# Attention, Mish MoE and SwiGLU MoE in one kernel: another order and other tiles for the conversion of the second MoE's weights

## The chip, the core and the metric

The kernel runs on one core of a Trainium2 chip. The metric is the device time of one execution in microseconds, median of the runs. The core has five engines with a queue of instructions each: TensorE (PE in the profile), VectorE (DVE), ScalarE (ACT), GpSimd (POOL) and SyncE (SP), which here issues every DMA. Each queue runs in the order in which the program wrote it; queues wait for one another only where a tile makes them.

## The reference

```python
def _attn_ref(q, k, v):            # 4 x 8 heads x 576 x 64; local heads and strided heads
...
    attn = attn / (np.sum(attn, axis=-1, keepdims=True) + 1e-09)
    return np.matmul(attn, v).astype(np.float32)

def _moe_ref(x, w_in, w_out):      # 2304 tokens, 512 -> 2048 -> 512
    h = x @ w_in
    sp = np.where(h > 20.0, h, np.log1p(np.exp(np.minimum(h, 20.0))))
    g = h * np.tanh(sp)
    return (g @ w_out).astype(np.float32)

def _moe2_ref(x, w_gate, w_val, w_out):   # 512 -> 1536 -> 512
    g = x @ w_gate
    silu = g * (1.0 / (1.0 + np.exp(-g)))
    val = x @ w_val
    return (silu * val @ w_out).astype(np.float32)
```

The weights come as 64-bit floats. The kernel itself turns them into 32-bit ones.

## The kernel before

**Precision.** Every operand of the two MoEs is held as two parts, hi (the value rounded to the matmul's type, by ScalarE, `split_hi`) and lo (the rest, a subtraction, `split_lo`), and each product is three matmuls (`mm3`): hi hi, hi lo, lo hi.

**Phases.** Attention runs first, its units interleaved with the start of MoE 1. MoE 1 is cut in 20 steps n = 0 to 19 (4 quarters of the hidden width by 5 chunks of tokens; four chunks have 512 tokens, the fifth, n = 4, 9, 14 and 19, has 256). Step n runs the first product of chunk n (`h`, four groups f of 12 matmuls each) and then the second product of chunk n-1 (`y`, 48 matmuls in four groups). The hidden PSUM tiles have the tag `mm` with three buffers, so group f = 3 needs the buffer that the Mish of group f = 0 (L436, ScalarE, out `u`) has read. After the second product four additions (L477, L479, `y_out`) go to VectorE. After step 19 come twelve rounds of MoE 2 (tiles `c..`, then `o`), which read their weights back from DRAM (`ld`, L555).

**Conversion of weights.** `wlist` holds 32 weight tiles of MoE 1 and 60 of MoE 2 (36 read from the input, 24 sums or differences `S12`, `S34` of tiles already converted). One unit of conversion is `w_unit`. For a tile read from the input it is: a Square of the high word on ScalarE (L183), four operations a, b, c, d on VectorE (L184, L187, L190, L193; d needs the Square), and the DMA that loads the raw tile of the unit two raw units on (`w_load`, L130; the tag `raw` has two buffers). For an S tile it is two half operations on VectorE (L165 and L171, or L167 and L174). Later `w_flush` makes the hi part (ScalarE, L74) and the lo part (GpSimd, L79), and for MoE 2 the DMA that stores both to DRAM (L142). For MoE 1 the parts stay in a tile of tag `w`; for MoE 2 they are built in a staging tile of tag `ws`, which has two buffers. The Square is written into the second half of the same tile, where the lo part comes later:

```python
    nc.scalar.activation(out=w[:, 1], in_=hi.bitcast(F32), func=AF.Square)
```

`w_unit` begins with `w_flush(1)`: unit k flushes all but the newest pending tile, so hi, lo and store of tile k-2 are written out ahead of the Square and of a to d of tile k.

**Where units stand.** Steps 3 to 17 of MoE 1 hold 82 units, 22 for MoE 1 and 60 for MoE 2 (`W1_STEP`, `W2_STEP`), placed after the groups of the two products by `bg`. `act_c` puts the hi part of the hidden values on ScalarE after each `y` group and its lo part on GpSimd (tile `g`). At the end of each step `w_flush()` makes the parts of all that is pending.

**Other tiles in the change.** `v` tiles of attention have four buffers (`NV`); the load of unit u+4 is issued after the product of unit u (`at_v`). In the rounds, the two hidden tiles of the last chunk (`fs4`) use the same tag. The output weights of each round (`p`) are loaded at the end of that round into tag `raw` (two buffers), and used by the `o` matmuls one round later.

Of the kernel before, what the change touches and what calls it, by code (L numbers as in the profile page):

```python
# [7 lines left out]
F32 = mybir.dt.float32  # L8
F32R = mybir.dt.float32r
# [3 lines left out]
ALU = mybir.AluOpType  # L13
# [32 lines left out]
    (2, 0, 18), (2, 1, 19), (2, 2, 20), (2, 3, 21), (3, 0, 21), (3, 1, 21), (3, 2, 21), (3, 3, 21),  # L46
)
WSTEPS = (0, 0, 1, 1, 1, 1, 1, 1, 1, 1, 1, 1, 1, 1, 1, 1) + (1, 2) * 6 + (0,) * 20
NV = 4
WF = 8  # L50
DO2 = 6

# [2 lines left out]
def local_strided_attention__mish_moe__swiglu_kernel(  # L55
# [22 lines left out]
    def split_lo(eng, lo, src, hi):  # L78
        eng.tensor_tensor(out=lo, in0=src, in1=hi.bitcast(F32), op=ALU.subtract)  # L79
# [52 lines left out]

    wpend = []

    def w_flush(keep=0):
        while len(wpend) > keep:
            key, w, tf = wpend.pop(0)
            split_hi(nc.scalar, w[:, 0], tf)
            split_lo(nc.gpsimd, w[:, 1], tf, w[:, 0])
            if len(key) == 3:  # L140
                wd[key] = dram.tile([128, 2, 512], F32, name="wd_%s_%d_%s" % key)
                nc.sync.dma_start(wd[key], w.bitcast(F32))  # L142

    def w_ops():
        i = wpos[1]
        if i >= len(wlist):
            return []
        wpos[1] += 1
        key, src = wlist[i]
        if len(key) == 2:  # L150
            t = sb.tile([128, 512], I32, tag="wtmp", name="wtmp", bufs=2)
            w = sb.tile([128, 2, 512], F32R, tag="w", name="w", bufs=10)
            wt[key] = w
        else:
            t = sb.tile([128, 512], I32, tag="pt", name="wt2", bufs=6)
            w = sb.tile([128, 2, 512], F32R, tag="ws", name="ws", bufs=2)
        tf = t.bitcast(F32)
        if src is None:
            t0, t1 = (f32[key[:2] + (x,)] for x in ("W0", "W1"))
            f32[key] = tf  # L160
            lo, hi = slice(0, 256), slice(256, 512)

            def s1():
                if key[2] == "S12":
                    nc.vector.tensor_tensor(out=tf[:, lo], in0=t1[:, lo], in1=t1[:, hi], op=ALU.add)  # L165
                else:
                    nc.vector.tensor_tensor(out=tf[:, lo], in0=t0[:, lo], in1=t1[:, lo], op=ALU.subtract)  # L167

            def s2():
                if key[2] == "S12":  # L170
                    nc.vector.tensor_tensor(out=tf[:, hi], in0=tf[:, lo], in1=t0[:, lo], op=ALU.subtract)  # L171
                else:
                    s = f32[key[:2] + ("S12",)]
                    nc.vector.tensor_tensor(out=tf[:, hi], in0=t0[:, hi], in1=s[:, hi], op=ALU.subtract)  # L174
                wpend.append((key, w, tf))

            return [s1, s2]
        raw = raws.pop(i).bitcast(I32).rearrange("p (n t) -> p n t", t=2)
        lo, hi = raw[:, :, 0], raw[:, :, 1]
        f32[key] = tf  # L180

        def a():
            nc.scalar.activation(out=w[:, 1], in_=hi.bitcast(F32), func=AF.Square)  # L183
            nc.vector.tensor_scalar(t, hi, 3, 0x3FFFFFFF, op0=ALU.logical_shift_left, op1=ALU.bitwise_and)  # L184

        def b():
            nc.vector.scalar_tensor_tensor(t, lo, 29, t, op0=ALU.logical_shift_right, op1=ALU.bitwise_or)  # L187

        def c():
            nc.vector.scalar_tensor_tensor(t, hi, -0x40000000, t, op0=ALU.bitwise_and, op1=ALU.bitwise_or)  # L190

        def d():
            nc.vector.scalar_tensor_tensor(tf, w[:, 1].bitcast(F32), SMALL2, tf, op0=ALU.is_ge, op1=ALU.mult)  # L193
            wpend.append((key, w, tf))
            w_load()

        return [a, b, c, d]
# [9 lines left out]
                wq.pop(0)()  # L207

    def w_unit():
        w_flush(1)  # L210
        for do in w_ops():
            do()


    pairs = [(b, hp) for b in range(B) for hp in ((0, 1, 2, 3) if b < B - 1 else (2, 3, 0, 1))]
# [3 lines left out]
        for j in range(0, nb, st_):  # L219
            units.append((i, b, hp, list(range(j, min(j + st_, nb)))))  # L220
    NU = len(units)
    qk_t, v_t = {}, {}
    st = {}

    def load_qk(i):
# [5 lines left out]

    def load_v(u):
        i, b, hp, js = units[u]
        t = sb.tile([128, 4, 128], F32, tag="v", name="v", bufs=NV)
        v_t[u] = t = t[:LK if hp < 2 else 128, :len(js)]
        nc.sync.dma_start(t, (v_loc if hp < 2 else v_str)[2 * b + hp % 2, u % 3, :, :len(js)])

# [132 lines left out]
            load_qk(i + 2)  # L370

    def at_v(u):
        if u + NV < NU:
            load_v(u + NV)

    DENSE = [
        [
# [67 lines left out]
    def do(n=None):  # L445
        for _ in range(len(todo) if n is None else min(n, len(todo))):
            todo.pop(0)()
# [52 lines left out]
    def g2_by_f(n, after, banks=PS4):  # L500
        nt = CHUNKS[n % NCH][1]
        y = [ps.tile([128, 512], F32, tag=t, name="y", bufs=k)[:, :nt] for t, k in banks]
        for f in range(QF):
            for e in range(4):
                g2_mm(n, y[e], e, f)
            after(f)
        for e in range(4):
            y_out(n, y[e], e)
# [35 lines left out]
    def ld(r, *what):  # L544
        if r >= 2 * NP:
            return
        P, i = divmod(r, NP)
        for x in what:
            for kind in "p" if x in (0, 1) else "gv":
                tag, n = TAGS[x]  # L550
                ws[kind, r, x] = t = sb.tile([128, 2, 512], F32R, tag=tag, name="wr", bufs=n)
                if x == "W1" and P == 1:
                    nc.sync.dma_start(t[:, :, 256:].bitcast(F32), wd[kind, i, x][:, :, 256:])
                else:
                    nc.sync.dma_start(t.bitcast(F32), wd[kind, i, x])  # L555
# [8 lines left out]
        ("X", "W1", 1, "T4"),  # L564
    ]
    BANK = {"g": {"X": ("mm", 3), "Y": ("mm", 3), "Z": ("mm", 3)}, "v": {"X": ("sc", 2), "Y": ("xp", 2), "Z": ("tp", 1)}}
    fv, fs = {}, {}

    def finish(r, f, c, w=512):
        t = fv.pop((r, f, c))  # L570
        if w == 512:
            h = sb.tile([128, 2, 512], F32R, tag="g", name="fs", bufs=6)
        else:
            h = sb.tile([128, 2, 256], F32R, tag="v", name="fs4", bufs=NV)
        split_hi(nc.scalar, h[:, 0], t)
        split_lo(nc.gpsimd, h[:, 1], t, h[:, 0])
        fs[r, f, c] = h
# [85 lines left out]
    with tc.manual_schedule():  # L663
# [75 lines left out]
        for n in range(3, NA):  # L739
            q, c = divmod(n, NCH)  # L740
            units = W1_STEP.get(n, 0) + W2_STEP.get(n, 0)
            left = [units, 8]

            def bg(k):
                while left[0] * 8 > units * k:
                    left[0] -= 1
                    w_unit()

            for f in range(QF):
                g1_open(n, f)  # L750
                for kc in range(4):
                    g1_mm(n, f, kc)
                act_a(n, f, False)
                bg(7 - f)
                if n == NA - 2 and f % 2:
                    operand(0, ("B11", "T1")[f // 2])

            def after(f):
                act_c(n, f)
                do()  # L760
                bg(3 - f)
                if n == NA - 2:
                    operand(0, ("T2", "B22", "T3", "B21")[f])
                if n == NA - 1 and f == 0:
                    operand(0, "T4")

            if n == NA - 1:
                w_flush()
                ld(0, "S34", "W0", "S12", "W1", 0, 1)
            g2_by_f(n - 1, after)  # L770
            w_flush()
        g2_by_f(NA - 1, lambda f: None, [("mm", 3), ("mm", 3), ("mm", 3), ("tp", 1)])
        for r in range(2 * NP + 1):
            P = r // NP
            if r < 2 * NP:
                ld(r + 1, "W0")

                def between(n):
                    if n == 2:
                        ld(r + 1, "S12")  # L780
                    if n == 4:
                        ld(r + 1, "S34")
                    if r == NP - 2 and n == 6:
                        operand(1, "B11")
                    if r == NP - 1 and n < 6:
                        operand(1, ("T1", "T2", "B22", "T3", "B21", "T4")[n])

                c_round(r, between)
            if r > 0:
                for t in range(4):  # L790
                    d_tile(r - 1, 1, t)
            if r < 2 * NP:
                finish(r, 0, 0)
                finish(r, 1, 0)
                if P == 0:
                    c4_round(r)
                ld(r + 1, "W1")
            if r > 0:
                for t in range(4):
                    d_tile(r - 1, 0, t)  # L800
                if r <= NP:
                    for t in range(2):
                        d_tile(r - 1, 4, t)
            if r > 0:
                ld(r, 0, 1)


_INS = ["qk", "v_loc", "v_str", "w1", "w2", "consts"]
# [86 lines left out]
```

## Time and profile before

| | |
|---|---|
| median of 3 runs | 992.34 us (987.35 to 992.46) |
| the profiled execution | 987.49 us, span 985.7 us |
| PE busy | 925.3 us (94%) |
| DVE busy | 616.2 us (63%) |
| ACT busy | 383.6 us (39%) |
| POOL busy | 374.4 us (38%) |
| mean granted TensorE clock | 0.967 |

The span is the time from the first to the last instruction. Busy shares are means over phases that differ: attention until about 166 us, steps 3 to 19 of MoE 1 until 561 us, then the rounds. A line number is a line of the kernel; all matmuls of the MoEs have one line (L83) and all hi and lo parts two (L74, L79), so tiles tell them apart.

### The profile page before, as it was taken

What the parts mean: (1) busy time and instruction counts of PE and PEld (TensorE: products, weight loads), DVE (VectorE), ACT (ScalarE), POOL (GpSimd) and SP (SyncE); (2) the same over time, 40 slices, a digit from 0 to 9 for tenths busy, and PEclk for the clock granted to TensorE, in tenths of its full rate; (3) what the DMA queues carried; (4) which work ended last, traced back from release to release, by engine and by line L of the source; (5) the groups of instructions that cost most, each with busy time, mean ns of one, the idle gap of its engine ahead of it and who ended that gap; (6) DMA issues with size and microseconds to landing.
All of it is one profiled execution on the core that took longest, in us unless ns stands there. A gap on an engine that the chain in (4) does not pass through costs nothing.

```text
span 985.7 us, 13926 instructions
## 1 busy us (share of the span) xinstructions
PE 925.3 (94%) x4982; PEld 767.8 (78%) x4987; DVE 616.2 (63%) x1232; ACT 383.6 (39%) x951; POOL 374.4 (38%) x303
## 2 busy tenths in 40 slices
PE   8998999997988969899599999999999899999997
PEld 6776887885867858678488888888887788888885
DVE  5896567698978989798886434333346343334433
ACT  5667646353434433443435343213224222322230
POOL 3345134664746646474556422021034221112210
PEclk9989999998989979899799999999999999999999
DMA  8774421454555455554442632523514246443313
GB/s 305 241 247 166 143 95 53 171 171 156 200 178 175 167 170 190 185 196 152 154 168 96 249 111 103 213 66 149 213 43 171 73 184 250 176 172 106 128 44 128
DMA packets 48501, 156.72 MB, mean 159 GB/s; under 512 B 5296, under 2 KB 11824, under 8 KB 48432
## 3 DMA queue, kind: packets, MB, share of 16 engines
q1 hardware_dynamic: 48432, 155.83, 44.9%
q8 instruction: 39, 0.64, 0.3%
q14 instruction: 30, 0.25, 0.1%
HBM read 119.64 MB, written 36.18 MB: 158 GB/s over the span
## 4 chain that ended last, share of the span: by engine, by line
PE 48%; ACT 2%; DVE 1%; issue 0%; DMA 0%; POOL 0%; ACTq 0%; POOLq 0%
PE o L83 15%; PE cXg L83 6%; PE cXv L83 6%; PE y L83 5%; PE c L83 4%; PE h L83 3%; PE cZv L83 3%; PE cZg L83 3%; PE cYv L83 2%; PE cYg L83 2%; ACT T L74 0%; DMA wr<-wd_p 0%; DVE T L79 0%; DVE B L79 0%; DVE k L616 0%
## 5 line engine op out<-in xcount | busy, mean ns | idle before, releaser
L83 PE MATMUL h<-xh,w 128*128 128x512 f32 (+1 forms) x640 | 210.3, 397 | 38.4 <-ACT u L436 38.0
L83 PE MATMUL y<-g,w 128*128 128x512 f32 (+1 forms) x960 | 208.0, 372 | 0.0
L83 PEld LDWEIGHTS y<-g,w 128*128 128x128 f32 x960 | 167.0, 190 | 29.8
L83 PEld LDWEIGHTS h<-xh,w 128*128 128x128 f32 x640 | 123.7, 200 | 64.1 <-ACT u L436 40.9
L83 PE MATMUL o<-wr,fs 128*128 128x512 f32 x648 | 152.3, 393 | 5.9 <-DMA wr<-wd_p 3.1
L79 POOL TENSOR_TENSOR fs<-k,fs 128x512 fp32r<-128x512 f32 x36 | 47.0, 1306 | 279.1 <-ACT fs L74 243.6
L83 PEld LDWEIGHTS o<-wr,fs 128*128 128x128 f32 x648 | 122.1, 189 | 32.4 <-DVE s L616 3.2
L79 POOL TENSOR_TENSOR g<-u,g 128x512 fp32r<-128x512 f32 (+1 forms) x80 | 111.4, 1399 | 83.8 <-ACT g L74 83.5
L83 PE MATMUL h<-xl,w 128*128 128x512 f32 (+1 forms) x320 | 124.1, 388 | 0.0
L659 DVE TENSOR_TENSOR acc<-acc,o 128x512 f32<-128x512 f32 x90 | 61.7, 687 | 62.4 <-PE o L83 62.4
L79 POOL TENSOR_TENSOR ws<-wt,ws 128x512 fp32r<-128x512 f32 x60 | 86.4, 1449 | 33.2 <-ACT ws L74 33.1
L278 ACT ACTIVATE pt<-pt,sm 108x64 f32<-108x64 f32 (+1 forms) x160 | 55.8, 350 | 50.1 <-DVE sm L263 49.8
L83 PEld LDWEIGHTS h<-xl,w 128*128 128x128 f32 x320 | 64.4, 201 | 9.2 <-DVE xl L79 0.3
L293 POOL TENSOR_TENSOR pt<-pt,sm 128x288 f32<-128x288 f32 (+2 forms) x48 | 37.1, 772 | 89.8 <-DVE sm L292 74.7
L183 ACT ACTIVATE ws<-raw 128x512 fp32r<-128x512 f32 x36 | 24.1, 670 | 118.4 <-issue 32.7
L603 DVE TENSOR_TENSOR k<-cZg,k 128x512 f32<-128x512 f32 x12 | 8.3, 691 | 98.4 <-PE cZg L83 98.4
L79 POOL TENSOR_TENSOR w<-wtmp,w 128x512 fp32r<-128x512 f32 x32 | 48.1, 1504 | 46.4 <-ACT w L74 40.4
L193 DVE SCALAR_TENSOR_TENSOR wt<-ws,wt 128x512 f32<-128x512 f32 x36 | 37.4, 1038 | 44.3 <-ACT ws L183 42.5
L74 ACT CAST fs<-k 128x512 fp32r<-128x512 f32 x36 | 22.4, 622 | 91.6 <-PE o L83 40.1
L83 PE MATMUL cXg<-T,wr 128*128 128x512 f32 x216 | 54.9, 390 | 0.4 <-DVE k L603 0.4
L83 PE MATMUL cXv<-T,wr 128*128 128x512 f32 x216 | 54.8, 389 | 0.0
L74 ACT CAST ws<-wt 128x512 fp32r<-128x512 f32 x60 | 36.3, 620 | 46.8 <-DVE wt L193 10.7
(96 smaller groups left out, 1526.3 us busy)
## 6 DMA issues: line engine op xcount, KB each, us to landing
raw<-in_w_dram SPq DMA_DIRECT2D x68, 512.0 KB, 3.7
qk<-in_qk_dram SPq DMA_DIRECT2D x16, 898.0 KB, 6.4
wr<-wd_g_S SPq DMA_DIRECT2D x24, 512.0 KB, 5.9
wr<-wd_v_S SPq DMA_DIRECT2D x24, 512.0 KB, 5.8
wr<-wd_p SPq DMA_DIRECT2D x24, 512.0 KB, 4.0
wr<-wd_g_W SPq DMA_DIRECT2D x18, 512.0 KB, 5.8
wr<-wd_v_W SPq DMA_DIRECT2D x18, 512.0 KB, 6.5
wd_g_W<-ws SPq DMA_DIRECT2D x12, 512.0 KB, 2.6
```

What stands on the lines that cost most here:

```text
L74: nc.scalar.copy(hi, src)
L79: eng.tensor_tensor(out=lo, in0=src, in1=hi.bitcast(F32), op=ALU.subtract)
L83: nc.tensor.matmul(o, lhsT=lhs, rhs=rhs, start=first and i == 0, stop=last and i == 2, skip_group_check=more)
L183: nc.scalar.activation(out=w[:, 1], in_=hi.bitcast(F32), func=AF.Square)
L193: nc.vector.scalar_tensor_tensor(tf, w[:, 1].bitcast(F32), SMALL2, tf, op0=ALU.is_ge, op1=ALU.mult)
L278: nc.scalar.activation(out=pt[:, jj], in_=pt[:, jj], func=AF.Exp, scale=-1.0, bias=sm[:, 0, jj:jj + 1], accum_out=sm[:, 1, jj:jj + 1],)
L293: nc.gpsimd.tensor_tensor(out=pt, in0=pt, in1=r.unsqueeze(2).to_broadcast([n, nb, w]), op=ALU.mult)
L603: nc.vector.tensor_tensor(out=t, in0=p, in1=t, op=ALU.add)
L659: nc.vector.tensor_tensor(out=acc[c][:, t], in0=acc[c][:, t], in1=o, op=ALU.add)
```

## The change

1. MoE 2's staging tiles alternate between the tags `ws` and `v`, two buffers each. The tag `v` now has two buffers of twice the size; attention's v tiles use them in pairs, and both loads of a pair (units u+3 and u+4) are issued after the product of an odd unit u. `fs4` tiles are paired in the same way.
2. For MoE 2 the Square goes to a scratch tile of its own, `sq`, of tag `pt`.
3. `w_unit` now begins with `w_lo(nc.vector)` and `w_hi()`: unit k writes out lo and store of tile k-2, then hi of tile k-1, then the Square and a to d of tile k.
4. In `w_unit`, and in the flushes from step 3 on, the lo part is on VectorE, for MoE 1's tiles too. The flushes during attention keep GpSimd.
5. The flush at the end of each step becomes `w_done()`, which flushes only if a tile of MoE 1 is pending; it is also called between the two products.
6. The `p` weights of the last round go to tag `w` and are loaded one round earlier.

```diff
@@ -46,7 +46,6 @@
     (2, 0, 18), (2, 1, 19), (2, 2, 20), (2, 3, 21), (3, 0, 21), (3, 1, 21), (3, 2, 21), (3, 3, 21),
 )
 WSTEPS = (0, 0, 1, 1, 1, 1, 1, 1, 1, 1, 1, 1, 1, 1, 1, 1) + (1, 2) * 6 + (0,) * 20
-NV = 4
 WF = 8
 DO2 = 6
 
@@ -132,14 +131,26 @@
 
     wpend = []
 
-    def w_flush(keep=0):
+    whalf = []
+
+    def w_lo(eng):
+        while whalf:
+            key, w, tf = whalf.pop(0)
+            split_lo(eng, w[:, 1], tf, w[:, 0])
+            if len(key) == 3:
+                wd[key] = dram.tile([128, 2, 512], F32, name="wd_%s_%d_%s" % key)
+                nc.sync.dma_start(wd[key], w.bitcast(F32))
+
+    def w_hi(keep=0):
         while len(wpend) > keep:
             key, w, tf = wpend.pop(0)
             split_hi(nc.scalar, w[:, 0], tf)
-            split_lo(nc.gpsimd, w[:, 1], tf, w[:, 0])
-            if len(key) == 3:
-                wd[key] = dram.tile([128, 2, 512], F32, name="wd_%s_%d_%s" % key)
-                nc.sync.dma_start(wd[key], w.bitcast(F32))
+            whalf.append((key, w, tf))
+
+    def w_flush(keep=0, eng=nc.gpsimd):
+        w_lo(eng)
+        w_hi(keep)
+        w_lo(eng)
 
     def w_ops():
         i = wpos[1]
@@ -153,7 +164,7 @@
             wt[key] = w
         else:
             t = sb.tile([128, 512], I32, tag="pt", name="wt2", bufs=6)
-            w = sb.tile([128, 2, 512], F32R, tag="ws", name="ws", bufs=2)
+            w = sb.tile([128, 2, 512], F32R, tag=("ws", "v")[i % 2], name="ws", bufs=2)
         tf = t.bitcast(F32)
         if src is None:
             t0, t1 = (f32[key[:2] + (x,)] for x in ("W0", "W1"))
@@ -178,9 +189,11 @@
         raw = raws.pop(i).bitcast(I32).rearrange("p (n t) -> p n t", t=2)
         lo, hi = raw[:, :, 0], raw[:, :, 1]
         f32[key] = tf
+        sq = w[:, 1].bitcast(F32) if len(key) == 2 else sb.tile([128, 512], F32, tag="pt", name="sq", bufs=6)
+        sqo = w[:, 1] if len(key) == 2 else sq
 
         def a():
-            nc.scalar.activation(out=w[:, 1], in_=hi.bitcast(F32), func=AF.Square)
+            nc.scalar.activation(out=sqo, in_=hi.bitcast(F32), func=AF.Square)
             nc.vector.tensor_scalar(t, hi, 3, 0x3FFFFFFF, op0=ALU.logical_shift_left, op1=ALU.bitwise_and)
 
         def b():
@@ -190,7 +203,7 @@
             nc.vector.scalar_tensor_tensor(t, hi, -0x40000000, t, op0=ALU.bitwise_and, op1=ALU.bitwise_or)
 
         def d():
-            nc.vector.scalar_tensor_tensor(tf, w[:, 1].bitcast(F32), SMALL2, tf, op0=ALU.is_ge, op1=ALU.mult)
+            nc.vector.scalar_tensor_tensor(tf, sq, SMALL2, tf, op0=ALU.is_ge, op1=ALU.mult)
             wpend.append((key, w, tf))
             w_load()
 
@@ -207,9 +220,14 @@
                 wq.pop(0)()
 
     def w_unit():
-        w_flush(1)
+        w_lo(nc.vector)
+        w_hi()
         for do in w_ops():
             do()
+
+    def w_done():
+        if any(len(x[0]) == 2 for x in wpend + whalf):
+            w_flush(0, nc.vector)
 
 
     pairs = [(b, hp) for b in range(B) for hp in ((0, 1, 2, 3) if b < B - 1 else (2, 3, 0, 1))]
@@ -219,7 +237,7 @@
         for j in range(0, nb, st_):
             units.append((i, b, hp, list(range(j, min(j + st_, nb)))))
     NU = len(units)
-    qk_t, v_t = {}, {}
+    qk_t, v_t, v_p = {}, {}, [None]
     st = {}
 
     def load_qk(i):
@@ -231,7 +249,9 @@
 
     def load_v(u):
         i, b, hp, js = units[u]
-        t = sb.tile([128, 4, 128], F32, tag="v", name="v", bufs=NV)
+        if u % 2 == 0:
+            v_p[0] = sb.tile([128, 2, 4, 128], F32, tag="v", name="v", bufs=2)
+        t = v_p[0][:, u % 2]
         v_t[u] = t = t[:LK if hp < 2 else 128, :len(js)]
         nc.sync.dma_start(t, (v_loc if hp < 2 else v_str)[2 * b + hp % 2, u % 3, :, :len(js)])
 
@@ -370,8 +390,10 @@
             load_qk(i + 2)
 
     def at_v(u):
-        if u + NV < NU:
-            load_v(u + NV)
+        if u % 2:
+            for x in (u + 3, u + 4):
+                if x < NU:
+                    load_v(x)
 
     DENSE = [
         [
@@ -547,7 +569,7 @@
         P, i = divmod(r, NP)
         for x in what:
             for kind in "p" if x in (0, 1) else "gv":
-                tag, n = TAGS[x]
+                tag, n = TAGS[x] if kind != "p" or r < 2 * NP - 1 else ("w", 10)
                 ws[kind, r, x] = t = sb.tile([128, 2, 512], F32R, tag=tag, name="wr", bufs=n)
                 if x == "W1" and P == 1:
                     nc.sync.dma_start(t[:, :, 256:].bitcast(F32), wd[kind, i, x][:, :, 256:])
@@ -564,14 +586,16 @@
         ("X", "W1", 1, "T4"),
     ]
     BANK = {"g": {"X": ("mm", 3), "Y": ("mm", 3), "Z": ("mm", 3)}, "v": {"X": ("sc", 2), "Y": ("xp", 2), "Z": ("tp", 1)}}
-    fv, fs = {}, {}
+    fv, fs, f4 = {}, {}, [None]
 
     def finish(r, f, c, w=512):
         t = fv.pop((r, f, c))
         if w == 512:
             h = sb.tile([128, 2, 512], F32R, tag="g", name="fs", bufs=6)
         else:
-            h = sb.tile([128, 2, 256], F32R, tag="v", name="fs4", bufs=NV)
+            if f == 0:
+                f4[0] = sb.tile([128, 2, 2, 256], F32R, tag="v", name="fs4", bufs=2)
+            h = f4[0][:, f]
         split_hi(nc.scalar, h[:, 0], t)
         split_lo(nc.gpsimd, h[:, 1], t, h[:, 0])
         fs[r, f, c] = h
@@ -765,10 +789,11 @@
                     operand(0, "T4")
 
             if n == NA - 1:
-                w_flush()
+                w_flush(0, nc.vector)
                 ld(0, "S34", "W0", "S12", "W1", 0, 1)
+            w_done()
             g2_by_f(n - 1, after)
-            w_flush()
+            w_done()
         g2_by_f(NA - 1, lambda f: None, [("mm", 3), ("mm", 3), ("mm", 3), ("tp", 1)])
         for r in range(2 * NP + 1):
             P = r // NP
@@ -801,8 +826,10 @@
                 if r <= NP:
                     for t in range(2):
                         d_tile(r - 1, 4, t)
-            if r > 0:
+            if 0 < r < 2 * NP - 1:
                 ld(r, 0, 1)
+            if r == 2 * NP - 2:
+                ld(r + 1, 0, 1)
 
 
 _INS = ["qk", "v_loc", "v_str", "w1", "w2", "consts"]
```

## Rows read from the trace of the kernel before

**Rows 1.** The page: busy time of TensorE, and in 40 equal slices the busy tenths of TensorE and VectorE.

```profile
PE 925.3 (94%) x4982; PEld 767.8 (78%) x4987; DVE 616.2 (63%) x1232; ACT 383.6 (39%) x951; POOL 374.4 (38%) x303
...
PE   8998999997988969899599999999999899999997
...
DVE  5896567698978989798886434333346343334433
```

**Rows 2.** Busy time of each engine in stretches: three single steps of MoE 1 (n = 5, 6 and 7), step 16, and last the whole of steps 3 to 17. Columns: from:to, its length, then busy us and (instructions) of PE, PEld, DVE, ACT and POOL, then the granted clock, the DMA share and GB/s.

```profile
205.13:221.76 16.63, 16.63 (x97) 14.76 (x96) 15.63 (x20) 7.76 (x14) 8.07 (x7) 1.00 0.50 159
221.76:253.13 31.37, 24.39 (x99) 19.66 (x97) 26.30 (x30) 11.35 (x21) 18.00 (x13) 0.89 0.46 151
253.13:274.89 21.76, 21.76 (x98) 18.02 (x96) 20.77 (x23) 8.43 (x15) 14.24 (x10) 1.00 0.61 218
...
460.27:495.11 34.84, 24.75 (x99) 19.86 (x97) 28.13 (x30) 11.07 (x20) 18.68 (x13) 0.80 0.44 151
...
166.71:517.15 350.44, 312.46 (x1441) 261.04 (x1440) 299.71 (x337) 140.25 (x259) 206.07 (x144) 0.93 0.49 172
```

**Rows 3.** Who waited for whom in steps 3 to 17: TensorE's one row, ScalarE's longest with its Square, VectorE's. Columns: total us, times, longest us.

```profile
PE h L83 <- ACT u L436: 38.0, 7, 10.1
...
ACT ws L183 <- issue: 32.7, 8, 5.3
ACT ws L183 <- DMA wd_p<-ws: 30.2, 3, 10.2
...
ACT ws L183 <- DMA raw<-in_w_dram: 17.5, 10, 2.9
...
DVE wt L193 <- ACT ws L183: 39.6, 17, 4.6
```

**Rows 4.** One such wait in order of time, step 16. Columns: start us, length us, engine, line, operation, out<-in, and in brackets the idle time before it and what ended it.

```profile
462.00 1.66 DVE L190 SCALAR_TENSOR_TENSOR wt<-raw,wt 128x512 int32<-128x512 int32 x1
...
464.18 0.36 SPq L142 DMA_DIRECT2D wd_p<-ws  x1
...
469.38 0.66 ACT L183 ACTIVATE ws<-raw 128x512 fp32r<-128x512 f32 x1 [9.90 <-DMA wd_p<-ws]
...
470.07 0.69 DVE L193 SCALAR_TENSOR_TENSOR wt<-ws,wt 128x512 f32<-128x512 f32 x1 [3.82 <-ACT ws L183]
...
478.07 0.59 ACT L436 ACTIVATE u<-h 128x512 f32<-128x512 f32 x1
...
478.72 0.79 PE L83 MATMUL h<-xh,w 128*128 128x512 f32 x1 [10.10 <-ACT u L436]
```

**Rows 5.** VectorE in order of time where GpSimd does nothing beside it: the first S12 halves, and one whole raw unit and the start of the next.

```profile
177.24 0.42 DVE L165 TENSOR_TENSOR wt<-wt 128x256 f32<-128x256 f32 x1
...
178.71 0.42 DVE L184 TENSOR_SCALAR wt<-raw 128x512 int32<-128x512 int32 x1
...
212.64 0.42 DVE L184 TENSOR_SCALAR wtmp<-raw 128x512 int32<-128x512 int32 x1
213.09 0.69 DVE L187 SCALAR_TENSOR_TENSOR wtmp<-raw,wtmp 128x512 int32<-128x512 int32 x1
...
215.23 0.42 DVE L184 TENSOR_SCALAR wtmp<-raw 128x512 int32<-128x512 int32 x1
```

**Rows 6.** Beside GpSimd: one stretch in which VectorE runs nine SBUF operations and GpSimd seven lo parts (columns as in rows 2), and GpSimd's and VectorE's groups of instructions in steps 3 to 17. Columns of a group: line, engine, operation, shape, count | busy us, mean ns of one | idle before.

```profile
247.12:258.94 11.82, 11.82 (x54) 9.79 (x53) 11.58 (x9) 3.97 (x7) 10.25 (x7) 1.00 0.43 150
...
L79 POOL TENSOR_TENSOR ws<-wt,ws 128x512 fp32r<-128x512 f32 x58 | 83.9, 1454 | 33.2 <-ACT ws L74 33.1
L79 POOL TENSOR_TENSOR g<-u,g 128x512 fp32r<-128x512 f32 x50 | 75.7, 1519 | 72.2 <-ACT g L74 72.2
L79 POOL TENSOR_TENSOR w<-wtmp,w 128x512 fp32r<-128x512 f32 x24 | 36.9, 1538 | 37.4 <-ACT w L74 31.4 <-PE h L83 5.6
...
L479 DVE TENSOR_TENSOR acc<-acc,y 128x512 f32<-128x512 f32 x36 | 22.2, 679 | 0.0
```

**Rows 7.** The nearest rows to a lo part on VectorE: in the rounds a VectorE operation with two SBUF inputs of the same size, and the lo parts of MoE 2's operands, each of which runs next to one on GpSimd (steps 18 and 19).

```profile
L616 DVE TENSOR_TENSOR k<-k,k 128x512 f32<-128x512 f32 x36 | 25.5, 708 | 4.1 <-DVE k L603 0.5
...
L79 DVE TENSOR_TENSOR B<-acc,B 128x512 fp32r<-128x512 f32 x3 | 3.9, 1316 | 3.1 <-ACT B L74 3.1
```

**Rows 8.** DMA issues by kind (KB each, median us from issue to landing), and for attention's v tiles the least, median and longest time to landing with the products of a unit and of the unit three later.

```profile
raw<-in_w_dram SPq DMA_DIRECT2D x68, 512.0 KB, 3.7
...
wr<-wd_g_S SPq DMA_DIRECT2D x24, 512.0 KB, 5.9
...
wd_p<-ws SPq DMA_DIRECT2D x12, 512.0 KB, 2.8
...
DMA to landing us min/median/max: 2.1/3.4/6.5
...
48.41 0.57 PE L334 MATMUL xp<-ts,v 96*64 96x64 f32 x12
...
57.68 0.91 PE L334 MATMUL xp<-ts,v 96*64 96x64 f32 x12
```

**Rows 9.** The end: TensorE's wait for the last round's output weights and what it ran then, and the stretch from the last `o` of round 10's weights to the end (columns as in rows 2).

```profile
968.79 1.37 PE L83 MATMUL o<-wr,fs 128*128 128x512 f32 x3 [2.65 <-DMA wr<-wd_p]
970.63 11.35 PE L83 MATMUL o<-wr,fs 128*128 128x512 f32 x45 [0.47 <-DMA wr<-wd_p]
...
966.16:985.70 19.54, 12.72 (x48) 9.64 (x48) 6.19 (x9) 0.00 (x0) 0.00 (x0) 0.91 0.44 161
```

## The prediction

> **What bounds the kernel now.** I read the page first [rows 1]: TensorE is busy 94% of the span, so only its idle and slow stretches can be won. The slices show where they are: between the 10th and the 20th, tenths of 5 to 8 lie beside full ones, and there VectorE stands at 7 to 9, while in the rounds behind it has mostly 3 to 6. That stretch is steps 3 to 17, the steps with units of conversion. I then cut it into single steps [rows 2]. A step without trouble takes 16.6 us when one of its products is of the short chunk (n = 4, 5, 9, 10, 14, 15) and 21.8 us otherwise: 6 x 16.63 + 9 x 21.76 = 295.6 us for the fifteen. They took 350.4, an excess of 54.8. The view of waits names 38.0 of it [rows 3]: TensorE stands seven times at the fourth group of a first product, because ScalarE has not yet read the PSUM tile of the first. The other 16.8 is the clock: in the disturbed steps the granted clock is 0.80 and 0.89 [rows 2], so part of the matmuls after such a wait run at 1.2 instead of 2.4 GHz, and each waited us costs 1.44 us (54.8 / 38.0).
>
> Why ScalarE is late is seen in order of time [rows 4]. Its queue stands 9.9 us at one Square, which writes into a staging tile that must first be stored. The store is issued at 464.2, after two things: the lo part on GpSimd, and the load ahead of it in SP's queue, which waits for operation c on VectorE. The Square starts 5.2 us after the issue. The Mish that TensorE needs is queued behind that Square and a second such one. The same Square holds VectorE, 39.6 us in 17 waits [rows 3].
>
> But VectorE is the second limit. In steps 3 to 17 it is busy 299.7 us [rows 2], and its own work is far less. A raw unit alone takes 215.23 - 212.64 = 2.59 us, two S units (178.71 - 177.24) / 2 = 0.74 each [rows 5]; the additions take 0.68 each [rows 6], 2.7 for a step (1.7 where the chunk is short). 58 x 2.59 + 24 x 0.74 + 12 x 2.7 + 3 x 1.7 = 205 us. The other 95 us are VectorE operations made longer by GpSimd's: 0.66 us for each of 144 GpSimd operations. Where VectorE has no pause it is more: in the stretch of 11.8 us [rows 6] its nine operations would take 4.9 us alone (four of 0.69, five of 0.42) and took 11.6, so 0.96 for each of seven.
>
> The Trainium skill, page "SBUF — State Buffer", section "Who interferes with whom", states this as a lock: a VectorE operation with two SBUF inputs and a GpSimd operation that reads SBUF block each other for a whole instruction. The rows agree: 0.69 alone, 1.66 beside GpSimd.
>
> **The change part by part.**
>
> *The Square's wait* goes. The scratch `sq` was last read by an earlier unit, three or more back by my count through the six `pt` buffers, and hi of tile k now meets a staging tile whose store was issued two units before, against 2.8 us to landing [rows 8]. What is late next is VectorE: hi of tile k-1 now stands at the head of unit k on ScalarE and waits for d of the unit just before, where `w_flush(1)` left one unit more. Behind it are queued the Square, the Mish and the hi parts of `g`. So TensorE will now wait for VectorE's lag alone, and the sum is VectorE's.
>
> *The lo parts.* 82 leave GpSimd. On VectorE one is not seen in these steps; the bounds are 0.7 (two SBUF inputs, same size) and 1.32 (always beside GpSimd) [rows 7]. I take 0.7 and count GpSimd's part separately, since GpSimd keeps only the 62 lo parts of `g`. For those the bounds are 0.66 and 0.96 each; VectorE will have few pauses, but some meet the additions, so 0.8.
>
> *VectorE by step*, against TensorE's 21.76 or 16.63. Raw unit 2.59 + 0.7 = 3.29, S unit 1.44, four `g` 3.2 (2.0 for the short chunk). `w_done` between the products makes VectorE wait for a hi part just issued; ScalarE's operations take about 0.6 [rows 4], some of it covered, 0.4 us in the eight steps that have it.
> - n = 6, 8, 11, 13, 16 (four raw, two S): 13.16 + 2.88 + 2.7 + 3.2 + 0.4 = 22.3, 0.6 too long. n = 7, 12 without the 0.4: 0.2.
> - n = 4, 9, 14 (three raw, two S): 9.87 + 2.88 + 2.7 + 2.0 = 17.4, 0.8 too long.
> - n = 5, 10 (five raw): 16.45 + 1.7 + 3.2 + 0.4 = 21.8, 5.1 too long. n = 15 (six raw): 25.0, 8.4.
> - n = 3 and 17 have room.
>
> The lag adds up to 5 x 0.6 + 2 x 0.2 + 3 x 0.8 + 2 x 5.1 + 8.4 = 24.4 us by step 16. TensorE doesn't feel the first 9: the Mish of the first group is due 3/8 of a long step in, 8.2 us, and ScalarE must have only d of the last unit but one by then (3.3 earlier), less three operations of its own (0.66 + 0.59 [rows 4] and a hi of that size). 15.4 us of waits remain, times 1.44 for the clock 22.2. Steps 3 to 17 take 295.6 + 22.2 = 318 us, 32.6 less. At steps 10 and 15 the lo of the last MoE 1 tile, now behind the additions on VectorE, lets only some 4 us of lag through; what is waited there is not waited later, and the sum stays.
>
> *The last weights.* Their slots in `w` are those of round 10's S12, done by then; SP's queue has only round 10's weights ahead. From 966.16 to 981.98 TensorE ran 48 matmuls [rows 9]; at 21.76 / 96 each [rows 2] they take 10.9. 4.9 us less.
>
> *Costed at nothing.* Attention's v loads: the first of a pair is issued three units ahead, not four; three units took 9.3 us, the longest load 6.5 [rows 8]. Without that cover, say behind a later product, at most 2 us a pair. `fs4` in pairs: the same bytes and order. SP's queue: the store of tile k-2 waits for a lo that VectorE does ahead of a of unit k, so the load behind it, which waits for c, is not held. ScalarE has as many operations as before. The pending tiles at step 19: two lo parts, 1.4 us, in steps that have room.
>
> The profiled execution took 987.5 us, as the lowest of three runs; the median is 992.3. 987.5 - 32.6 - 4.9 = **950.0 us**, which I keep for the median too.
>
> **The rivals.**
>
> *TensorE alone bounds.* If a `g` costs VectorE 0.66 and the wait after `w_done` is covered, the thirteen steps 4 to 16 are 0.56 shorter each (7 us) and eight of them another 0.4 (3 us): lag 14, 5 above what is let through, 7 with the clock. 54.8 - 7 + 4.9 = 53 less, 935; with nothing left, 928. For it: GpSimd's operations will bunch behind the second product, near the additions. Against: the saturated stretch, 0.96.
>
> *The raw loads.* There are still two raw tiles, and each load waits for c of the unit two before: 3.7 to landing and some 2 of a to c and issue is 6 us for two raw units, where VectorE needs 6.6. If landing rises to the 5.9 of the `wr` loads, issued several at a time [rows 8], it is 8.2, 0.8 a unit: over the 16 raw units of steps 5, 10 and 15, 13 us, times 1.44: 969. For it: ScalarE waited 17.5 us for raw tiles already [rows 3]. Against: only in ten short waits.
>
> *Slower.* If VectorE's lost time does not leave with GpSimd's operations, because a moved lo takes 1.32 like the rows beside GpSimd, its work grows by 82 x 0.62 = 51 us. 73 of these units lie in steps 4 to 16: lag 24.4 + 45, less 9, times 1.44 is 87 us: 295.6 + 87 = 383, 32 above now; less the tail's 4.9, 1015. It decides where a lo costs VectorE over 1.0: there the extra lag passes 22.6 us, times 1.44 the whole 32.6. Against: `k<-k,k`, 0.71, has both inputs in SBUF. The Trainium skill, page "Perfetto Trace Analysis", section "Optimizing Scalar/DVE Operations", speaks for this rival: as the two engines share a read port, moving work between them might not help. By the rows, an operation on GpSimd takes up to 0.96 from VectorE and one on VectorE 0.7.
>
> *No change.* The first term is eaten whole and only the tail is won, 982 and up: a lo near 1.0.
>
> **How the numbers follow.** Forecast, 940 to 962: 0.55. TensorE alone, under 940: 0.18. Raw loads or another wait of VectorE, 962 to 982: 0.15. No change: 0.05. Slower: 0.07. A measurement of this kernel can tell about 0.5% (the three runs spread by that). The first three are faster: 0.88, 0.05, 0.07. The range leaves out the slower end and the best of the TensorE case: 930 to 975.
>
> **What would show it.** Right: no Square waiting for a store; `ws` and `w` gone from GpSimd's groups; their VectorE rows near 0.7 and those of a to d nearer 0.42 and 0.69; VectorE at 9 tenths or more in steps 5 to 16; TensorE's waits for `u` halved and placed at steps 10, 11, 15 and 16; no wait for `wr<-wd_p` at the end. Wrong: lo rows above 1.0, VectorE idle for raw tiles, or a new wait in attention.

## The result and the profile after

The changed kernel takes **939.84 us** (median of four runs, 939.29 to 941.43) where the kernel before took 990.41 beside it; the ratio is 0.949 (95% interval 0.946 to 0.953). The profiled execution took 941.43 us, its span is 939.4. The forecast was 950 with a range of 930 to 975.

The page first: busy time, the slices of TensorE and VectorE and the granted clock.

```profile
PE 910.8 (97%) x4982; PEld 757.0 (81%) x4987; DVE 612.1 (65%) x1314; ACT 382.9 (41%) x951; POOL 258.0 (27%) x221
...
PE   8988999999999999999999999999998999999998
...
DVE  5896565998999999999967323424447253334434
...
PEclk9998999999999999999999999999999999999999
```

TensorE's gaps between the 10th and the 20th slice are closed [rows 1], and VectorE stands at nine tenths there, but for the 10th at eight. Steps 3 to 17 whole, then steps 5, 6, 10, 11, 14, 15 and 16 (columns as in rows 2).

```profile
168.52:475.75 307.23, 300.00 (x1441) 251.63 (x1440) 293.24 (x418) 141.36 (x262) 93.46 (x65) 0.99 0.56 197
206.94:223.57 16.63, 16.63 (x97) 14.76 (x96) 14.07 (x23) 8.12 (x15) 1.78 (x2) 1.00 0.45 143
223.57:245.36 21.79, 21.79 (x99) 18.03 (x97) 20.84 (x32) 10.06 (x18) 8.15 (x6) 1.00 0.58 204
...
306.23:324.98 18.75, 16.92 (x98) 14.68 (x96) 17.90 (x29) 8.94 (x17) 1.93 (x3) 1.00 0.51 168
324.98:347.51 22.53, 22.36 (x98) 17.88 (x97) 21.58 (x30) 9.73 (x18) 7.34 (x6) 1.00 0.58 202
...
391.03:409.93 18.90, 17.18 (x98) 14.88 (x97) 18.40 (x27) 8.50 (x18) 6.91 (x6) 1.00 0.54 205
409.93:430.29 20.36, 18.52 (x98) 15.83 (x97) 19.47 (x30) 9.37 (x17) 3.53 (x4) 0.92 0.55 184
430.29:453.99 23.70, 22.45 (x98) 17.87 (x97) 22.79 (x33) 11.29 (x21) 6.96 (x5) 1.00 0.58 201
```

Steps 3 to 17 take 307.2 us in place of 350.4 [rows 2], 43.2 less, and 11.6 above the 295.6 that TensorE needs. Step 6 has lost all of its 9.6 us of excess, step 16 11.1 of 13. The rounds take 419.3 instead of 424.2, 4.9 less. Steps 18 and 19 are the same to 0.1, and step 3 starts 1.8 later. 43.2 + 4.9 - 1.8 = 46.3, the difference of the spans.

Who waits in steps 3 to 17: all of TensorE's, all of VectorE's, and ScalarE's longest.

```profile
PE h L82 <- DVE w L78: 3.7, 2, 1.8
PE y L82 <- DVE acc L501: 1.4, 2, 1.0
PE y L82 <- DVE w L78: 1.4, 2, 1.2
PE h L82 <- ACT u L458: 0.7, 1, 0.7
...
DVE wt L206 <- ACT sq L196: 2.0, 2, 1.6
DVE wt L206 <- DVE wt L203: 0.5, 1, 0.5
DVE wt L197 <- DMA raw<-in_w_dram: 0.4, 1, 0.4
DVE ws L78 <- ACT ws L73: 0.4, 1, 0.4
...
ACT ws L73 <- DVE wt L206: 77.3, 33, 4.1
```

The 38.0 us for the Mish are 0.7 [rows 3]; no Square waits for a store. TensorE waits 7.2 us, nearly all of it for VectorE itself. VectorE waits 3.3 us in 307. The direction has turned: ScalarE now waits for VectorE's operation d (77.3 us), where VectorE had waited for ScalarE's Square. VectorE is the full engine, and TensorE follows it closely.

VectorE's new lo parts and its operation d, and the most of what GpSimd has left (the rest are twelve short lo parts of `g` and two lo parts of `w` at the start):

```profile
L78 DVE TENSOR_TENSOR ws<-wt,ws 128x512 fp32r<-128x512 f32 x58 | 42.4, 731 | 1.1 <-ACT ws L73 0.4
L206 DVE SCALAR_TENSOR_TENSOR wt<-sq,wt 128x512 f32<-128x512 f32 x36 | 40.5, 1125 | 5.9 <-ACT sq L196 2.0 <-DVE wt L203 0.5
...
L78 DVE TENSOR_TENSOR w<-wtmp,w 128x512 fp32r<-128x512 f32 x22 | 14.8, 686 | 0.0
...
L78 POOL TENSOR_TENSOR g<-u,g 128x512 fp32r<-128x512 f32 x51 | 79.3, 1565 | 176.2 <-ACT g L73 176.1
```

And six rows of VectorE in order of time: first the additions of step 3; then those of step 7, which start 5.3 us into step 8, and behind them d, a lo, and a of the next unit; last the additions of step 16.

```profile
189.92 2.48 DVE L499 COPY acc<-y 128x512 f32<-128x512 f32 x4
...
272.39 2.47 DVE L501 TENSOR_TENSOR acc<-acc,y 128x512 f32<-128x512 f32 x4
...
277.36 0.69 DVE L206 SCALAR_TENSOR_TENSOR wtmp<-w,wtmp 128x512 f32<-128x512 f32 x1
277.96 0.69 DVE L78 TENSOR_TENSOR ws<-wt,ws 128x512 fp32r<-128x512 f32 x1
278.57 0.42 DVE L197 TENSOR_SCALAR wtmp<-raw 128x512 int32<-128x512 int32 x1
...
461.39 2.47 DVE L501 TENSOR_TENSOR acc<-acc,y 128x512 f32<-128x512 f32 x4
```

A lo lasts 0.69 us, but 0.61 after its start the next operation starts; four additions take 2.47. Both matter below.

### The profile page after: what moved, and what is told of

Same layout as the page of the kernel before. It is cut to its first block, busy times and chain, and to the rows that moved or that the text cites. A ratio compares the mean times of both kernels' runs of the same rounds, so it can differ in the third digit from the quotient of the medians.

```text
span 939.4 us, 13955 instructions
## 1 busy us (share of the span) xinstructions
PE 910.8 (97%) x4982; PEld 757.0 (81%) x4987; DVE 612.1 (65%) x1314; ACT 382.9 (41%) x951; POOL 258.0 (27%) x221
## 4 chain that ended last, share of the span: by engine, by line
PE 65%; DVE 27%; ACT 4%; issue 2%; DMA 1%; POOL 0%; SPq 0%; DVEq 0%; ACTq 0%; POOLq 0%
PE o L82 15%; PE y L82 9%; PE h L82 9%; PE cXg L82 7%; PE cXv L82 7%; PE c L82 4%; DVE wt L206 3%; PE cZv L82 3%; PE cZg L82 3%; DVE ws L78 3%; DVE wt L200 3%; DVE wt L203 3%; DVE acc L501 2%; PE sc L271 2%; DVE wtmp L203 2%
## 5 line engine op out<-in xcount | busy, mean ns | idle before, releaser
L82 PE MATMUL h<-xh,w 128*128 128x512 f32 (+1 forms) x640 | 199.6, 381 | 4.8 <-DVE w L78 3.7
L82 PEld LDWEIGHTS h<-xh,w 128*128 128x128 f32 x640 | 117.8, 191 | 27.3 <-DVE w L78 4.5
L82 PE MATMUL h<-xl,w 128*128 128x512 f32 (+1 forms) x320 | 119.4, 373 | 0.0
L73 ACT CAST ws<-wt 128x512 fp32r<-128x512 f32 x60 | 37.3, 622 | 97.9 <-DVE wt L206 77.3
L82 PEld LDWEIGHTS h<-xl,w 128*128 128x128 f32 x320 | 61.3, 192 | 8.6 <-DVE xl L78 0.3
L624 ACT COPY k<-cXg 128x512 f32<-128x512 f32 x24 | 14.1, 589 | 85.9 <-PE cXg L82 85.9
L82 PEld LDWEIGHTS cXg<-T,wr 128*128 128x128 f32 x216 | 40.5, 188 | 9.2 <-DVE k L627 0.9
L458 ACT ACTIVATE u<-h 128x512 f32<-128x512 f32 (+1 forms) x68 | 36.3, 541 | 27.6 <-PE h L82 27.5
L82 PEld LDWEIGHTS cXv<-T,wr 128*128 128x128 f32 x216 | 40.5, 188 | 8.4
```

Of the source, the lines that this page charges most:

```text
L73: nc.scalar.copy(hi, src)
L82: nc.tensor.matmul(o, lhsT=lhs, rhs=rhs, start=first and i == 0, stop=last and i == 2, skip_group_check=more)
L458: nc.scalar.activation(out=u, in_=p, func=AF.Mish)
```

## The experiments

The theory at this point: two limits lay on one another, the Square that waited for a store, and VectorE's time, of which GpSimd's operations took a large part. The rivals are that one of them was everything. Each kernel below was timed beside the kernel before on the same chip; between chips the kernel before differs by up to 2 us (medians of 989.0 to 991.1), and differences between kernels of different chips are uncertain by as much.

**One part at a time.** Lo parts back on GpSimd in the changed kernel:

```diff
     def w_unit():
-        w_lo(nc.vector)
+        w_lo(nc.gpsimd)
         w_hi()
...
-            w_flush(0, nc.vector)
+            w_flush(0, nc.gpsimd)
...
```

> The changed kernel with all 82 lo parts of the weights put back on GpSimd; order, staging tiles, scratch and last weights stay changed. Theory (two limits: the Square's wait, and VectorE's time, of which each GpSimd operation takes 0.8 to 0.9 us and a lo on VectorE 0.62): VectorE's own work in steps 3 to 17 falls from 252 to 202 us, but 144 instead of 65 GpSimd operations lengthen it by 112 to 127 us, so 314 to 329 where the changed kernel has 307; with TensorE's clock the steps take 315 to 335 and the kernel 948 to 967. Rival (the Square's wait was everything, and where the lo parts run is indifferent): 938 to 942.

The kernel before with the lo parts of the weights on VectorE alone:

```diff
...
     def w_unit():
-        w_flush(1)
+        w_flush(1, nc.vector)
...
```

> The kernel before with the 82 lo parts of the weights on VectorE and nothing else changed: two staging tiles, the Square in the staging tile, the old order, the old last weights. Theory (the Square still waits for a store, which now waits for VectorE's lo): the wait stays, VectorE idles in it as before; 968 to 990. Rival (VectorE's time was the only limit, the Square's wait just filled its pauses): the gain of the steps comes nearly whole, 942 to 955.

The kernel before with the scratch for the Square alone:

```diff
...
-            nc.scalar.activation(out=w[:, 1], in_=hi.bitcast(F32), func=AF.Square)
+            nc.scalar.activation(out=sqo, in_=hi.bitcast(F32), func=AF.Square)
...
```

> The kernel before with the Square of MoE 2's tiles in a scratch tile and nothing else changed: two staging tiles, the old order, lo parts on GpSimd. Theory (the Square's wait goes, VectorE's lost time stays): TensorE's waits for u fall by half or less, no Square waits for a store, VectorE has no pause; 955 to 972. Rival 1 (the Square's wait was everything): 942 to 948, which is the changed kernel without its tail. Rival 2 (two staging tiles are too few, so the hi part takes over the Square's wait): 980 to 990.

And, later, both of these together in the kernel before:

> The kernel before with both parts at once: the Square in a scratch tile and the 82 lo parts of the weights on VectorE; two staging tiles, the old order, the old last weights. Theory 1 (the two parts alone gave 16.0 and 17.9 us and add up, the rest of the changed kernel's gain is order and staging): 953 to 960. Theory 2 (each frees what the other left, so together they give nearly the whole gain but the tail's 4.9): 943 to 949. Theory 3 (with lo on VectorE right behind its hi, VectorE now waits for ScalarE, and the order was needed): 960 to 972.

| kernel | us | ratio to before | steps 3 to 17 |
|---|---|---|---|
| lo back on GpSimd | 953.57 | 0.964 (0.960 to 0.968) | 320.0 |
| lo on VectorE alone | 971.82 | 0.982 (0.978 to 0.985) | 332.6 |
| scratch alone | 973.67 | 0.983 (0.980 to 0.987) | 333.2 |
| scratch and lo | 956.46 | 0.966 (0.963 to 0.970) | 317.2 |

Neither part is everything. With the lo parts back on GpSimd the changed kernel loses 13.7 us. Each part alone gives about a third of the gain, and together they add up (16.0 + 17.9 = 33.9 expected, 32.6 measured). The waits of the two kernels with one part each, first lo on VectorE alone (ScalarE, VectorE, TensorE), then scratch alone (TensorE, and ScalarE's two longest for stores):

```profile
ACT ws L183 <- DMA wd_p<-ws: 25.0, 3, 8.5
...
DVE wt L193 <- ACT ws L183: 30.2, 21, 3.2
...
PE h L83 <- ACT u L436: 23.5, 7, 7.3
```

```profile
PE h L83 <- ACT u L438: 27.4, 9, 7.0
...
ACT ws L74 <- DMA wd_g_W<-ws: 12.2, 6, 2.1
ACT ws L74 <- DMA wd_g_S<-ws: 12.2, 5, 4.6
```

With lo on VectorE alone the Square still waits for stores, up to 8.5 us at a time. With the scratch alone no Square does, but VectorE, with GpSimd's operations beside it, is busy 308 us, more than the 295.6 that TensorE needs. The forecast for the scratch was 1.7 us too good at its upper end, and TensorE's waits for `u` fell from 38.0 to 27.4 us, not to half. The hi parts wait 49.0 us for stores here; in the kernel before it was 17.7, and 64.1 for the Square. So they took over about half of the Square's wait, as the second rival had it in part.

**What a GpSimd operation costs.** All lo parts of steps 3 to 19 on VectorE, the hidden values' too:

```diff
-        todo.insert(1, lambda: split_lo(nc.gpsimd, g[:, 1, :nt], u, g[:, 0, :nt]))
+        todo.insert(1, lambda: split_lo(nc.gpsimd if n < 3 else nc.vector, g[:, 1, :nt], u, g[:, 0, :nt]))
```

> The changed kernel with the 62 lo parts of the hidden values (g) of steps 3 to 19 on VectorE too, so that GpSimd does next to nothing there. Theory (a GpSimd operation takes 0.8 us from VectorE, the same on VectorE 0.62): VectorE's work in steps 3 to 17 falls by some 12 us to about 293, TensorE's waits nearly go, 928 to 935. Rival (VectorE's lost time isn't GpSimd's doing): 38 us more work on a full engine, times the clock's share, 970 to 990.

Each lo part of the hidden values computed twice on GpSimd:

> The changed kernel with each lo part of g of steps 3 to 19 computed twice on GpSimd (the second writes the same values again). It measures what one GpSimd operation costs where VectorE is full. Theory: 60 more of them in steps 3 to 17 at 0.8 to 0.96 us of VectorE each are 48 to 58 us more on the full engine, with TensorE's clock up to 1.44 of that: steps 3 to 17 go from 307 to 350 to 390 us, the kernel to 985 to 1023. Rival (0.5 us each, as the busy times alone suggest): 965 to 985. Rival (nothing, GpSimd has room): 940.

Steps 3 to 17 of the first, and of the second (columns as in rows 2):

```profile
167.77:463.57 295.80, 295.80 (x1442) 250.78 (x1440) 275.86 (x480) 143.44 (x262) 7.95 (x5) 1.00 0.59 205
```

```profile
167.99:520.42 352.43, 311.74 (x1442) 255.94 (x1440) 340.10 (x413) 139.51 (x259) 170.44 (x122) 0.97 0.48 170
```

The first takes **928.72 us** (ratio 0.939, 0.935 to 0.942), less than the kernel before and the changed one. VectorE has 62 operations more than in the changed kernel and is busy 17 us less; TensorE has no wait at all in these steps, which take 295.8 us, the 295.6 of the prediction. Its groups on VectorE show where the time was:

```profile
L200 DVE SCALAR_TENSOR_TENSOR wt<-raw,wt 128x512 int32<-128x512 int32 x36 | 25.9, 720 | 1.2
L203 DVE SCALAR_TENSOR_TENSOR wt<-raw,wt 128x512 int32<-128x512 int32 x36 | 25.9, 719 | 1.2
```

These are b and c, 1.05 and 1.02 us before (the groups at L187 and L190), 0.72 now. The second kernel takes 987.04 us, 0.996 of before: nearly all of the gain is gone. 60 GpSimd operations more made the steps 45.2 us longer, 0.75 us each (12 of them are the short chunk's). The price of 0.8, and 0.5 for the short ones, makes 48 x 0.8 + 12 x 0.5 = 44.4. The clock adds nothing to it: VectorE sets the pace, busy 340 of 352 us. The theory's upper half, which had the clock added, was wrong.

**Staging tiles and order.** Two staging tiles in the changed kernel:

```diff
-            w = sb.tile([128, 2, 512], F32R, tag=("ws", "v")[i % 2], name="ws", bufs=2)
+            w = sb.tile([128, 2, 512], F32R, tag="ws", name="ws", bufs=2)
```

> The changed kernel with two staging tiles (tag ws alone) in place of four; everything else stays changed. Theory (the hi part of tile k stands one unit earlier than before, so with two tiles it meets the store of tile k-2, issued only a unit ahead, and ScalarE waits for landings again): waits of the hi part for a store of 1 to 3 us in most units of the 60, part of them before a Mish; 944 to 962. Rival (two are enough once the Square is elsewhere, the other two are spare): 938 to 942.

The same in the kernel with all lo parts on VectorE:

> The changed kernel with every lo part of steps 3 to 17 on VectorE (as in the run with 928.7 us) and two staging tiles in place of four. Theory (the hi parts wait for stores as in the run with two tiles, but VectorE has some 12 us of room and takes the delay up): 929 to 934, no or few waits of TensorE. Rival (the waits for stores pass through ScalarE to TensorE whatever VectorE has): 938 to 945.

The old order within a unit, everything else changed:

```diff
     def w_unit():
-        w_lo(nc.vector)
-        w_hi()
+        w_flush(1, nc.vector)
```

> The changed kernel with the old order within a unit: unit k writes out hi, lo and store of tile k-2 (lo on VectorE) ahead of its Square and a to d; four staging tiles, scratch, w_done and the last weights stay changed. Theory A (four tiles are worth something only with the order that writes hi a unit earlier; with the old one lo stands right behind its hi and VectorE waits for ScalarE): 945 to 953, the run with scratch and lo alone less the tail. Theory B (the four tiles carry the gain, the order none): 937 to 943.

They take 952.71, 941.00 and 947.12 us. In the first, ScalarE waits for stores again, now with the hi part:

```profile
ACT ws L73 <- DMA wd_v_W<-ws: 20.3, 9, 3.8
ACT ws L73 <- DMA wd_g_S<-ws: 13.4, 4, 4.7
```

That costs 12.9 us. (The forecast had such waits in most of the 60 units; they are 15.) The order alone, with two tiles, is worth nothing (952.7 against 956.5 less the tail's 4.9); four tiles with the old order (and `w_done`) are worth 4.5 (947.1 against 951.6); both together 12. The order moves hi a unit nearer to the store that its tile needs, so it only pays with the tiles. In the old order with four tiles theory A's time is right but its reason is not shown: VectorE waits only 5 us for hi parts, and TensorE's longest waits are for the additions (5.8 us). Why just these come later there is left open.

The second was my miss: I thought that a VectorE with room would take the delay up. TensorE's waits in it, VectorE's longest and ScalarE's longest for a store:

```profile
PE h L82 <- DVE w L78: 7.0, 2, 3.7
PE y L82 <- DVE w L78: 1.6, 1, 1.6
...
DVE g L78 <- ACT g L73: 18.1, 8, 3.3
...
ACT ws L73 <- DMA wd_g_S<-ws: 19.8, 7, 6.8
```

VectorE has room, 275 us busy of 307, but stands behind ScalarE, which stands at hi parts waiting for stores (56.6 us in all); its queue is in order, so the last weights of MoE 1 come late at steps 10 and 15. The room didn't help while the engine waited.

**The last weights.** The old place and tag for the last round's output weights:

> The changed kernel with the last round's output weights loaded at the old place and into the old tag. Theory: the wait for them at the end comes back, 4.9 us, 943 to 947, all of it in the rounds (419.3 to 424.2 us from the first product of MoE 2 to the end). Rival (the tail was won elsewhere): 938 to 942.

946.94 us, inside the forecast; the rounds take 423.8 us again, 4.5 more than in the changed kernel, with the old wait (2.7 us at the end). That is near the 4.9 costed. The profiled executions differ by 5.5 us (the medians by 7.1): steps 3 to 17, where the code is the same, took 1.4 us longer, so kernels can differ by that much there without a cause in their code.

**Waited twice or once?** The flush of steps 4, 9 and 14 ahead of the additions:

```diff
             after(f)
+        done()
         for e in range(4):
             y_out(n, y[e], e)
...
-            g2_by_f(n - 1, after)
-            w_done()
+            g2_by_f(n - 1, after, done=w_done)
```

> The changed kernel with the flush at the end of steps 4, 9 and 14 written ahead of VectorE's four additions in place of behind them, so that the last weights of MoE 1 are ready 2.5 us earlier at steps 5, 10 and 15. Theory A (a wait there is a wait saved later, as the prediction had it): the two waits of 1.8 us go and come back as waits for u or for the additions in steps 11 to 16, 938 to 942. Theory B (they are lost by themselves): 933 to 937.

942.36 us, not better, and 0.4 above theory A's range. Its steps 10 and 11, then 15 and 16, and TensorE's longest waits:

```profile
306.09:322.72 16.63, 16.63 (x98) 14.76 (x96) 15.80 (x25) 7.04 (x13) 1.29 (x2) 1.00 0.49 161
322.72:347.53 24.81, 22.67 (x98) 17.80 (x97) 23.75 (x34) 11.65 (x21) 7.97 (x6) 1.00 0.60 202
409.92:426.55 16.63, 16.63 (x97) 14.76 (x96) 15.79 (x25) 7.05 (x13) 1.29 (x2) 1.00 0.55 169
426.55:455.41 28.86, 24.97 (x98) 20.02 (x97) 27.73 (x40) 13.98 (x25) 9.87 (x7) 0.88 0.57 200
...
PE h L82 <- ACT u L458: 5.7, 3, 3.9
```

Steps 10 and 15 are free of waits, 2.1 and 3.7 us shorter; steps 11 and 16 are 2.3 and 5.2 longer, and waits for `u` have gone from 0.7 to 5.7 us. Theory A's mechanism holds: a wait of TensorE for a lagging VectorE is time in which VectorE catches up.

## Why the prediction was right

The change made the kernel faster by 46 us in the profiled executions, where 37.5 were forecast. The difference is 10.6 us too many that were forecast for steps 3 to 17, less the 1.8 by which step 3 starts later. By the medians the gain is 50.6: the forecast of 950 started from the lowest of three runs, 987.5, and from their median, 992.3, the same terms give 954.8. That 950 lies no farther from the measured time is in part the luck of this choice. By its own steps:

- **The bound, 295.6 us for steps 3 to 17:** right. It was reached to 0.2 us once VectorE had room.
- **The Square's wait goes, and VectorE is late next:** right. The scratch alone shows the first; ScalarE's 77.3 us of waits for d show the second.
- **A lo on VectorE 0.7, not 1.32:** right, 0.73 and 0.69. The rival *slower* needed 1.0.
- **A lo of `g` on GpSimd 0.8 of VectorE's time** (0.73 on the mean with the short ones, 38 us for the 52 in steps 4 to 16): near, by two readings. Doubling it gave 0.75, short ones included. In the changed kernel it was more: from the additions at the end of step 3 to those at the end of step 16 VectorE takes 271.5 us; at the median spacing of the same operations in the kernel with all lo parts on VectorE they would take 223.7; less 2.0 of waits, 45.7 are left, 0.88 for each of the 52. Operation d was to come nearer to 0.69 and went from 1.05 to 1.13. Why the added ones cost less is not shown. The Trainium skill, page "SBUF — State Buffer", section "Who interferes with whom", gives the reason, a port pair held for a whole instruction; the two kernels agree, with VectorE's operations at 0.72 where GpSimd stands still. Moving a lo to VectorE gives back 0.75 or more for 0.61.
- **VectorE's lag by step, and the clock on top of it:** the mechanism held, but the size was off, and this is the term that failed. Forecast were 24.4 us of lag by step 16, of which 9 are let through; the other 15.4 were to be waits, with the clock 22.2. Measured are 11.6: 7.2 of waits, and 4.4 in which TensorE ran slower (granted clock 0.92 in step 15). For steps 4 to 16 TensorE alone needs 252.1 us (6 x 16.63 + 7 x 21.76). VectorE, from the additions behind step 3 to those behind step 16, takes 271.5 (189.92 to 461.39, shown above). So the lag was 19.4; 7.8 was let through, and 11.6 lengthened TensorE's steps, its slower stretches included. The clock's share was no addition: while TensorE runs slower VectorE catches up, as it does while TensorE waits. Of the 10.6 us too many, the factor 1.44 made 6.8 and the lag 5.0, less the 1.2 that was let through too little.
- **What was wrong in the lag itself:** its 5.0 us is what two larger errors left of each other, which was luck. VectorE's own operations were costed some 12 us too dear, since I had added their lengths where their spacing counts: a lo is 0.61 after which the next starts, not 0.7 (73 in steps 4 to 16: 6.6 us); the additions take 2.47, not 2.7 (3 us); and the wait behind `w_done`, 0.4 in eight steps, is 0.4 us in all (3 us). GpSimd's part was 45.7 instead of 38, 7.7 too cheap. By step, the additions in VectorE's queue start 4.7 us after the end of step 9 and 8.5 after that of step 10, which was itself 2.1 longer than TensorE needs, so in this five-raw step VectorE needed 5.9 more than TensorE against 5.1 forecast; the six-raw step 15 is 9.1 against 8.4. The long steps came out shorter than summed: the additions start 6.2 us after the end of step 5, 5.5 after that of step 6, 5.3 and 5.6 after 7 and 8, and this lag should have grown by 0.2 to 0.6 each time.
- **Where TensorE would wait:** the steps were right, 10, 11, 15 and 16; 0.4 us in step 9 and 1.7 in step 14 came besides. The reason was right in part. The 3.7 us at steps 10 and 15 are for the last lo parts of MoE 1's tiles, a place that the prediction had named. Another 1.4, in 11 and 16, are for such lo parts too, 1.4 in 9 and 14 for additions, and only 0.7, in step 14, for `u`, which was to be the sign. In steps 9 and 14 the first product is short, so the second product needs the first of the additions some 5.2 us into the step (those behind step 8 start 5.6 us into step 9, and TensorE waits 0.4); that I had not seen.
- **What is waited there is not waited later:** right, shown by moving the flush. The same holds for the time that the slow clock costs, and the factor 1.44 went against it.
- **The tail, 4.9:** right, 4.9 between the two kernels and 4.5 by putting the old place back.
- **At nothing:** raw loads, 0.4 us of VectorE's waits and none of ScalarE's long ones: that rival fell. Attention: step 3 starts at 168.5 us, 166.7 before. That is not shown to be the v loads' doing: with the old v loads it started at 168.5 and 169.7 (lo on VectorE alone, scratch alone), with the new ones at 167.8 to 171.3 (all lo parts on VectorE, two staging tiles).
- **The four staging tiles** were costed together with the Square's wait; that they are worth 12.9 us because the new order needs them was not priced.

The measured time lies at the border of the forecast and of the rival *TensorE alone*. Of this rival's two reasons one held (no wait behind `w_done`), the other did not: `g` was not cheaper.

## What to carry to other kernels

Before an operation is moved between GpSimd and VectorE, find a stretch where both are full and divide what VectorE's operations are longer there by the number of GpSimd operations: that price, not GpSimd's own duration, is what the move gives back. Sum an engine's work by the spacing of its instructions, not by their lengths, when its total lies within a few per cent of the bound. Where that engine sets the pace, don't put TensorE's slow clock on top of TensorE's waits: its lag already holds both. And when a buffer's wait is removed by writing part of the work earlier, count the buffers again for the new order.

## What was not expected

Two staging tiles cost 12 us even where VectorE had 20 us of room (busy 276 of 296; 941.0 against 928.7): the room was of no use behind a queue that waited. And the kernel with all these lo parts on VectorE has GpSimd busy 8 us in 296 and TensorE at the full clock throughout: leaving an engine idle was the fastest arrangement measured.
